# Interleaving the first two token blocks of an attention and mixture-of-experts kernel: one list of units, PSUM banks by role, a new order before the first unit

## The chip, the core and the metric

The kernel runs on one core of one Trainium2 chip. The metric is the device time of one execution in microseconds (us). Each kernel was executed several times; the median stands for it.

## What is computed

Inputs are attention tensors q, k, v of 8 batches, 8 heads, 576 positions and 64 features, and the weights of two layers. The output has 4608 tokens (8 × 576) of 512 features. The reference, cut to what matters:

```python
q_s = exp(q - max(q, -1)); q_s /= sum(q_s, -1) + 1e-9
k_s = exp(k - max(k, 2));  k_s /= sum(k_s, 2) + 1e-9      # over the 576 positions
kv = einsum('bhsd,bhse->bhde', k_s, v)
x = einsum('bhsd,bhde->bhse', q_s, kv)                    # then as [4608, 512]
h = x @ w_in;  g = h * cos(h);  x = g @ w_out             # 512 -> 2048 -> 512
keep = x @ w_skip > 0
e = argmax(x[keep] @ w_gate)                              # one of 8 experts a token
x[keep] += prob[e] * (maximum(x[keep] @ w1[e], 0) @ w2[e])
```

## The kernel before

**Blocks and units.** The 4608 tokens are cut into NB = 12 blocks of TB = 384. A block goes through the middle layer in NC = 16 units, one for each chunk of 128 of the 2048 features. Unit n of block j and chunk c has `h_mm` (L323: twelve products of 384 columns, in three terms of high and low parts of weight and x, four pieces of features), a chain that makes h·cos(h) (L328 and L329 in `chain_a`; L333, L334, L335 in `chain_b`; L340 and L342 in `chain_c`), and `out_mm` (L351: nine products of 512 columns, three groups of tokens by three terms), which adds into three PSUM banks of the block. `out_mm` follows LAG = 3 units behind. L335 is the last to read the PSUM bank of a unit's h. L328 and L333, L334, L340 run on ScalarE, L329 and L335 on VectorE, L342 on GpSimd.

**Weights.** w_in and w_out come as 64-bit numbers, in 32 chunks of 512 KB in the list `order`. A call of `w_step` takes one chunk to float32 and, two steps later, splits it into a high part (L141, ScalarE) and a low part (L150, on VectorE, or on GpSimd for chunks in the list LOP); L146 (ScalarE), L147 and L152 (VectorE) and L153 (GpSimd) convert the bits. There are 34 steps, three ahead of the first unit; each also issues the load of the chunk seven places later in `order`. In block 0 the tables WA, WB, WC say at which unit and at which place of it a step is taken. All weights stay in SBUF after that.

**Attention.** The x of block j + 1 is made while the units of block j run, by `attention`, which puts the pieces at units by tables (A1, Q1, X1 for block 1, AT and others for later ones): `kmax_a`, `kmax_b`, `kmax_c` (maximum of k and its subtraction, L200 to L217), `k_exp`, `kv_mm` (L231 to L237), `q_max` (L246, L247), `q_exp` (L250), `q_norm` (L255 to L261), `q_trans` (transposes, L298) and `x_make` (L310 to L314). From block 2 on the transposes of q are made by DMAs and VectorE (`q_block`, `q_turn`). A new batch of k and v begins in some blocks only; block 2 needs none. The exponential (L221, L250) needs another ScalarE table than the sine of the chain.

**Routing.** The routing of block j − 1 (`x2_trans` or `x2_block` and `x2_turn`, `logits` L392, `gates` L400, `rank`, `gate_exp`, `weigh`, and three table writes `place` L454 of GpSimd) runs during block j. The experts' products come after the last block.

**What sets the order.** The program is scheduled by hand: each engine runs its instructions in the order in which this code writes them, and SyncE issues the loads and stores in that order too. PSUM has eight banks of 512 numbers a partition: three for `out_mm`, a pool of three for h, a pool of two for all else.

## Time and profile before

| | us |
|---|---|
| median of three runs | 1286.64 (1280.89 to 1287.6) |
| the profiled execution, span from first to last instruction | 1285.2 |
| TensorE matmuls busy | 1216.3 (95%) |
| weight loads of TensorE busy | 1070.6 (83%) |
| VectorE busy | 772.6 (60%) |
| ScalarE busy | 739.0 (57%) |
| GpSimd busy | 412.2 (32%) |

The busy shares are averages over the whole span; stretches of it differ, so they are read by windows of time. Times in the trace count from the first instruction. An idle time in brackets says how long the engine stood before the instruction and what it waited for last.

### The profile page before, as it was taken

The page shows a single profiled execution, that of the slowest core. Times are in us where ns is not written, and L with a number is a line of the kernel's source. Part 1 is how long each engine was busy: PE and PEld are TensorE (multiplying, and loading weights), DVE is VectorE, ACT ScalarE, POOL GpSimd, SP SyncE. Part 2 cuts the span into 40 slices and gives each one's busy share as a digit, 9 for nine tenths or more (in the row PEclk, how much of TensorE's full clock was granted, in tenths as well). Part 3 has the DMA queues.
Part 4 walks back from the last instruction along what each step waited for, and adds up shares of the span by engine and source line. Part 5 has one row for each costly group of instructions (what it writes and reads, how often), then busy time and mean ns, then how long its engine had stood idle before and what let it go on. Part 6 is the DMA issues. An engine that isn't in the chain of part 4 may idle for free. (4 is left out here: it accounts for less than half of the span.)

```text
span 1285.2 us, 19966 instructions
## 1 busy us (share of the span) xinstructions
PE 1216.3 (95%) x7046; PEld 1070.6 (83%) x7046; DVE 772.6 (60%) x1539; ACT 739.0 (57%) x1432; POOL 412.2 (32%) x365
## 2 busy tenths in 40 slices
PE   7768999999999999999999999999999799999976
PEld 3666888888898998989888888988888688999964
DVE  7999635565553556554355655435577566767747
ACT  3657655665665566556556655656575355555436
POOL 3666632324333242333324233333110212221311
PEclk8989999999999999999999999999999899999988
DMA  9910222234222123322222232220336567776746
GB/s 303 369 63 1 64 37 62 50 70 104 63 62 38 62 53 85 86 63 66 34 62 53 64 106 63 64 36 16 109 86 204 167 195 244 225 233 215 230 143 202
DMA packets 215230, 143.03 MB, mean 111 GB/s; under 512 B 139322, under 2 KB 178490, under 8 KB 215104
## 3 DMA queue, kind: packets, MB, share of 16 engines
q1 hardware_dynamic: 209856, 129.33, 36.1%
q0 software_dynamic: 5248, 12.17, 2.8%
q8 instruction: 61, 1.00, 0.4%
q14 instruction: 65, 0.53, 0.1%
HBM read 110.94 MB, written 16.08 MB: 99 GB/s over the span
## 5 line engine op out<-in xcount | busy, mean ns | idle before, releaser
L323 PE MATMUL h<-xh,w 128*128 128x384 f32 x1536 | 435.3, 345 | 21.0 <-POOL w L150 6.2
L351 PE MATMUL o<-w,gh 128*128 128x512 f32 x1152 | 363.1, 396 | 2.3 <-ACT x L363 2.3
L323 PEld LDWEIGHTS h<-xh,w 128*128 128x128 f32 x1536 | 284.0, 190 | 38.3 <-DVE w L150 7.0
L342 POOL TENSOR_TENSOR gl<-a,gh 128x384 fp32r<-128x384 f32 x176 | 184.2, 1047 | 402.2 <-ACT gh L340 294.5
L323 PE MATMUL h<-xl,w 128*128 128x384 f32 x768 | 261.5, 340 | 0.1
L351 PEld LDWEIGHTS o<-w,gh 128*128 128x128 f32 x1152 | 214.7, 189 | 39.1 <-ACT x L363 3.6
L351 PE MATMUL o<-w,gl 128*128 128x512 f32 x576 | 228.7, 397 | 1.5 <-POOL gl L342 1.5
L335 DVE SCALAR_TENSOR_TENSOR a<-a,h 128x384 f32<-128x384 f32 x192 | 104.6, 545 | 192.1 <-ACT a L334 192.1
L328 ACT ACTIVATE a<-h 128x384 f32<-128x384 f32 x192 | 93.1, 485 | 181.1 <-PE h L323 108.3
L329 DVE SCALAR_TENSOR_TENSOR a<-a,h 128x384 f32<-128x384 f32 x192 | 105.3, 549 | 138.5 <-ACT a L328 138.4
L121 DVE TENSOR_TENSOR w<-wr,w 128x512 fp32r<-128x512 f32 x224 | 144.1, 687 | 12.5 <-ACT w L120 6.6
L323 PEld LDWEIGHTS h<-xl,w 128*128 128x128 f32 x768 | 146.1, 190 | 5.4 <-DVE xl L314 0.4
L340 ACT CAST gh<-a 128x384 fp32r<-128x384 f32 x192 | 97.9, 510 | 72.0 <-DVE a L335 71.9
L772 PE MATMUL h<-xh,w 128*128 128x256 f32 x704 | 138.5, 282 | 0.0
L351 PEld LDWEIGHTS o<-w,gl 128*128 128x128 f32 x576 | 108.5, 188 | 29.2 <-POOL gl L342 2.6
L120 ACT CAST w<-wr 128x512 fp32r<-128x512 f32 x224 | 126.4, 619 | 8.7 <-DMA wr<-in_w 7.0
L772 PEld LDWEIGHTS h<-xh,w 128*128 128x128 f32 x704 | 114.3, 190 | 3.8 <-ACT w L120 0.4
L783 PE MATMUL o<-w,gh 128*128 128x512 f32 x352 | 114.0, 405 | 0.0
L333 ACT ACTIVATE a<-a 128x384 f32<-128x384 f32 x192 | 100.7, 525 | 11.0 <-DVE a L329 10.7
L334 ACT ACTIVATE a<-a 128x384 f32<-128x384 f32 x192 | 100.8, 525 | 6.1
L775 ACT ACTIVATE gh<-h 128x256 fp32r<-128x256 f32 x88 | 33.8, 384 | 120.2 <-PE h L772 96.1
L772 PE MATMUL h<-xl,w 128*128 128x256 f32 x352 | 99.2, 282 | 0.0
(197 smaller groups left out, 1505.3 us busy)
## 6 DMA issues: line engine op xcount, KB each, us to landing
wr<-in_w SPq DMA_DIRECT2D x112, 512.0 KB, 4.5
qt<-in_q SPq DMA_DIRECT2D x12, 768.0 KB, 6.7
out<-x SPq DMA_DIRECT2D x36, 256.0 KB, 2.2
wr<-in_w_in SPq DMA_DIRECT2D x16, 512.0 KB, 10.1
wr<-in_w_out SPq DMA_DIRECT2D x16, 512.0 KB, 11.0
xl<-x SPq DMA_DIRECT2D x160, 48.0 KB, 2.1
xh<-qt SPq DMA_DIRECT2D x160, 48.0 KB, 2.1
vt<-in_v SPq DMA_DIRECT2D x7, 1040.0 KB, 6.1
```

Of the source, the lines that this page charges most:

```text
L120: nc.scalar.copy(hi, src)
L121: nc.vector.tensor_tensor(lo, src, hi.bitcast(F32), op=ALU.subtract)
L323: nc.tensor.matmul(Hp[n], win(a, kk, c), xT[j][b][:, kk, :], start=t == 0, stop=t == len(seq) - 1)
L329: nc.vector.scalar_tensor_tensor(a, a, MAGIC, Hp[n], op0=ALU.subtract, op1=ALU.subtract)
L333: nc.scalar.activation(a, a, AF.Sin, scale=PI)
L334: nc.scalar.activation(a, a, AF.Square)
L335: nc.vector.scalar_tensor_tensor(a, a, 0.5, Hp.pop(n), op0=ALU.subtract, op1=ALU.mult)
L340: nc.scalar.copy(G[n]["h"], a)
L342: eng.tensor_tensor(G[n]["l"], a, G[n]["h"].bitcast(F32), op=ALU.subtract)
L351: nc.tensor.matmul(O[j][g], gg[a][:, g * P:(g + 1) * P], wout(b, c), start=c == 0 and t == 0, stop=c == NC - 1 and t == 2)
L772: nc.tensor.matmul(ps, win2(a, kk, c0, c * P, P), xt[b][:, kk, 0:T2], start=t == 0, stop=t == len(seq) - 1)
L783: nc.tensor.matmul(o[g], g_[a][:, g * P:(g + 1) * P], wout(b, c0 + c), start=c == 0 and t == 0, stop=c == NF - 1 and t == 2)
```

## The change

Blocks 0 and 1 no longer run one after the other. The list UNITS names block and chunk of every unit: four units of block 0, then a unit of block 1 and one of block 0 in turn, then the rest; from block 2 on the order is the old one. `h_mm` and `out_mm` read block and chunk from it, and the loop counts along it.

The attention of block 1 is moved in front of unit 4 (`attention_head`), at the first four units; block 2's attention lies between units 12 and 31. The weight steps go by one short table WS (1, 2, 2, 2, 2, 1, then one at every unit), all at one place of a unit. The loads of k, v and q of block 1 are issued before the first unit. The routing of block 0 moves into block 2, where it runs beside block 1's, and its transposes are made on TensorE.

PSUM is one pool of eight named banks, and `roles` says which are for `out_mm` of a block, for h and for the rest: first 0 to 2, 3 to 5, 6 and 7. From unit 4 on, with two blocks open, `out_mm` of block 1 has 5 to 7, h has 3 and 4, and nothing is left for the rest; after block 0's last `out_mm` it is 5 to 7, then 3, 4 and 0, then 1 and 2.

Ahead of the first unit, the order of work is another: fewer warm-up products, `kmax_c` and `k_exp` of the first half of k directly after `kmax_b`, and the subtraction of q's maximum and half of q's scaling on VectorE for block 0.

```diff
-A1 = (3, 3, 4, 6, 7, 9, 9, 9, 10, 8)
...
+HEAD = 4
+UNITS = [(0, c) for c in range(HEAD)]
+for _c in range(10):
+    UNITS += [(1, _c), (0, HEAD + _c)]
+UNITS += [(0, 14), (1, 10), (0, 15)] + [(1, _c) for _c in range(11, NC)]
+UNITS += [(_j, _c) for _j in range(2, NB) for _c in range(NC)]
+POS = {u: n for n, u in enumerate(UNITS)}
+LAST0, LAST1 = POS[0, NC - 1], POS[1, NC - 1]
+KQ = 12, 2, 2
...
+WS = (1, 2, 2, 2, 2, 1)
...
+    banks, used = {}, {"h": 0, "m": 0}
+
+    def roles(o, h, m):
+
+        banks.update(o=o, h=h, m=m)
+
+    def bank(b):
+        return pp.tile([P, 512], F32, tag=f"b{b}", name=f"b{b}")
+
+    def turn_of(kind):
+        used[kind] += 1
+        return bank(banks[kind][used[kind] % len(banks[kind])])
...
+    roles((0, 1, 2), (3, 4, 5), (6, 7))
...
-        nc.gpsimd.tensor_tensor(t, t, m[:, :, None].to_broadcast([P, NG * H, D]), op=ALU.subtract)
+        eng = nc.gpsimd if j else nc.vector
+        eng.tensor_tensor(t, t, m[:, :, None].to_broadcast([P, NG * H, D]), op=ALU.subtract)
...
     def h_mm(n):
-        j, c = divmod(n, NC)
-        Hp[n] = ps_h.tile([P, TB], F32, tag="h", name="h")
+        j, c = UNITS[n]
+        Hp[n] = hidden()
...
-        if j < NB - 2:
+        if 0 < j < NB - 2:
             f[2] = [(x2_block, (j,))]
             f[TURN] = [(x2_turn, (j,))]
...
+    def attention_head():
+
+        f = {}
+        add = lambda s, fn, *a: f.setdefault(s, []).append((fn, a))
+        for c in range(1, 5):
+            add((0, 0, 1, 1)[c - 1], kmax_a, 1, 0, NP, (c,))
+        add(0, x_new, 1)
+        add(0, q_max, 1)
+        add(1, kmax_b, 1)
+        add(1, q_exp, 1)
+        add(1, kmax_c, 1)
+        add(2, k_exp, 1)
+        add(2, q_norm, 1)
+        add(3, kv_mm, 1)
+        for i in range(NP):
+            add(3, q_trans, 1, i)
+            add(3, x_make, 1, i)
+        add(KQ[0] - 4, load_q, 2)
+        add(KQ[0], q_max, 2)
+        add(KQ[0] + 1, q_exp, 2)
+        add(KQ[0] + 2, q_norm, 2)
+        add(KQ[0] + 4, q_block, 2)
+        add(KQ[0] + 8, q_turn, 2)
...
         for n in range(N + LAG):
-            j, c = divmod(n, NC)
-            if c == 0:
+            j, c = UNITS[n] if n < N else (NB, n - N)
+            if n == POS[1, 0]:
+                roles((5, 6, 7), (3, 4), ())
...
+                if j == 2:
+                    early0 = routing(0, rp, (0, 1, 2, 2, 3, 4, 5, 6, 7, 8))
...
+                jo, co = UNITS[n - LAG]
+                if co == NC - 1:
+                    evac(jo, xp)
+                    if jo == 0:
+                        roles((5, 6, 7), (3, 4, 0), (1, 2))
+            if at[0] < len(order) + 2:
+                w_step(WS[n] if n < len(WS) else 1)
```

**VectorE at the first units.** Names: wr, u and w are a chunk of weights on its way, a the chain, h its PSUM tile (b_ and a number in the new kernel), kt, km and kmx block 1's k and its maximum, qt and qm its q. Before, behind the second unit:

```order
L335 SCALAR_TENSOR_TENSOR a<-a,h 128x384
L329 SCALAR_TENSOR_TENSOR a<-a,h 128x384
L147 TENSOR_SCALAR u<-wr 128x512
L150 TENSOR_TENSOR w<-u,w 128x512
L152 SCALAR_TENSOR_TENSOR wr<-wr,u 128x512
L147 TENSOR_SCALAR u<-wr 128x512
L150 TENSOR_TENSOR w<-u,w 128x512
L152 SCALAR_TENSOR_TENSOR wr<-wr,u 128x512
L335 SCALAR_TENSOR_TENSOR a<-a,h 128x384
```

In the changed kernel, behind its second unit:

```order
L362 SCALAR_TENSOR_TENSOR a<-a,b_357 128x384
L356 SCALAR_TENSOR_TENSOR a<-a,b_391 128x384
L166 TENSOR_SCALAR u<-wr 128x512
L169 TENSOR_TENSOR w<-u,w 128x512
L171 SCALAR_TENSOR_TENSOR wr<-wr,u 128x512
L166 TENSOR_SCALAR u<-wr 128x512
L169 TENSOR_TENSOR w<-u,w 128x512
L171 SCALAR_TENSOR_TENSOR wr<-wr,u 128x512
L219 TENSOR_TENSOR km<-km,kt 128x512
L219 TENSOR_TENSOR km<-km,kt 64x512
L227 TENSOR_REDUCE kmx<-b_436 128x4
L235 TENSOR_TENSOR kt<-kt,b_444 128x2048
```

Two weight steps stand between two units in both; the maximum and subtraction of block 1's k have come in behind them.

**TensorE where block 1's x is made.** Names: qt and qh, ql are q and its split transpose, kvbh and kvbl the split product of k and v, m a PSUM tile of the small pool, o the sums of `out_mm`. Before, transposes and products (L298, L310) lie between units:

```order
L310 MATMUL m_1168<-qh_1034,kvbh0_91 128x192
L310 MATMUL m_1168<-ql_1035,kvbh0_91 128x192
L310 MATMUL m_1168<-qh_1034,kvbl0_92 128x192
L310 MATMUL m_1168<-qh_1034,kvbh1_93 128x192
L310 MATMUL m_1168<-ql_1035,kvbh1_93 128x192
L310 MATMUL m_1168<-qh_1034,kvbl1_94 128x192
L298 MATMUL m_1177<-ident_58,qt_492 128x128 x3
L323 MATMUL h_1193<-xh_284,w_1120 128x384
```

In the changed kernel, the end of four such pairs, ahead of the fifth unit (the first of block 1):

```order
L337 MATMUL b_649<-qh,kvbl_88 128x192
L325 MATMUL b_658<-ident,qt 128x128 x3
L337 MATMUL b_666<-qh,kvbh_85 128x192
L337 MATMUL b_666<-ql,kvbh_85 128x192
L337 MATMUL b_666<-qh,kvbl_86 128x192
L337 MATMUL b_666<-qh,kvbh_87 128x192
L337 MATMUL b_666<-ql,kvbh_87 128x192
L337 MATMUL b_666<-qh,kvbl_88 128x192
L350 MATMUL b_675<-xh,w 128x384
```

Each transpose now stands directly ahead of the products that read it, with no unit between.

**TensorE in the interleaved part.** Here b with a digit is the PSUM bank: b3 and b4 hold h, b0 to b2 sums of block 0, b5 to b7 sums of block 1.

```order
L350 MATMUL b3_815<-xh_296,w_707 128x384
L350 MATMUL b3_815<-xl_297,w_707 128x384
...
L378 MATMUL b5_838<-w_424,gh_750 128x512
...
L378 MATMUL b7_840<-w_424,gl_751 128x512
L350 MATMUL b4_860<-xh_386,w_414 128x384
L350 MATMUL b4_860<-xl_387,w_414 128x384
...
L378 MATMUL b0_525<-w_805,gh_792 128x512
```

Before, at this place, all units were of block 0 and h went round three banks; now units of both blocks alternate and h alternates between two banks.

## Rows read from the trace of the kernel before

**Rows 1.** Busy time by stretch: length, engines with instruction counts, granted clock, DMA share, GB/s.

```profile
34.00:140.00 106.00, 81.02 (x439) 68.67 (x438) 101.41 (x133) 69.66 (x133) 72.92 (x56) 0.92 0.38 133
140.00:211.00 71.00, 71.00 (x364) 63.34 (x364) 34.95 (x77) 43.97 (x86) 26.07 (x23) 1.00 0.19 34
```

**Rows 2.** Timeline of TensorE: start, us, engine, line, operation, tiles, count, idle time before.

```profile
33.78 0.34 PE L323 MATMUL h<-xh,w 128*128 128x384 f32 x1
...
46.90 0.44 PE L323 MATMUL h<-xh,w 128*128 128x384 f32 x1 [3.83 <-DVE a L335]
...
50.49 0.79 PE L351 MATMUL o<-w,gh 128*128 128x512 f32 x2
...
139.82 0.34 PE L323 MATMUL h<-xh,w 128*128 128x384 f32 x1
...
144.03 0.34 PE L323 MATMUL h<-xh,w 128*128 128x384 f32 x1
...
209.52 0.34 PE L310 MATMUL m<-qh,kvbh 128*128 128x384 f32 x1
...
210.58 0.34 PE L323 MATMUL h<-xh,w 128*128 128x384 f32 x1
```

**Rows 3.** Timeline of VectorE, first chain operation, then two weight steps and a chain.

```profile
36.65 0.55 DVE L329 SCALAR_TENSOR_TENSOR a<-a,h 128x384 f32<-128x384 f32 x1 [1.30 <-ACT a L328]
...
118.67 0.41 DVE L147 TENSOR_SCALAR u<-wr 128x512 uint32<-128x512 uint32 x1
...
120.70 0.41 DVE L147 TENSOR_SCALAR u<-wr 128x512 uint32<-128x512 uint32 x1
...
123.09 0.54 DVE L335 SCALAR_TENSOR_TENSOR a<-a,h 128x384 f32<-128x384 f32 x1
123.55 0.54 DVE L329 SCALAR_TENSOR_TENSOR a<-a,h 128x384 f32<-128x384 f32 x1
```

**Rows 4.** Timeline of VectorE ahead of the first unit.

```profile
11.08 3.00 DVE L200 TENSOR_TENSOR km<-kt 128x256 f32<-128x256 f32 x1
...
14.45 1.21 DVE L216 TENSOR_TENSOR kt<-kt,m 128x1024 f32<-128x1024 f32 x1
...
17.62 0.42 DVE L208 TENSOR_REDUCE kmx<-m 128x2 f32<-128x256 f32 x1 [0.84 <-PE m L206]
```

**Rows 5.** Timeline of TensorE, transposes and products that make x of block 0.

```profile
22.54 0.82 PE L298 MATMUL h<-ident,qt 128*128 128x128 f32 x6
...
25.86 0.44 PE L310 MATMUL m<-ql,kvbh 128*128 128x384 f32 x1 [1.42 <-DVE ql L121]
...
31.42 0.69 PE L310 MATMUL m<-qh,kvbh 128*128 128x384 f32 x1
...
32.82 0.52 PE L310 MATMUL m<-qh,kvbh 128*128 128x384 f32 x1
```

**Rows 6.** Timeline of ScalarE, a table load and the exponential behind it.

```profile
97.28 1.28 ACT L250 ACT_TABLE_LOAD   x1
98.58 1.48 ACT L250 ACTIVATE qt<-qt 128x1536 f32<-128x1536 f32 x1
```

**Rows 7.** Timelines of VectorE and GpSimd, a step with nothing beside it, one beside GpSimd.

```profile
85.33 0.41 DVE L147 TENSOR_SCALAR u<-wr 128x512 uint32<-128x512 uint32 x1
...
86.87 0.54 DVE L335 SCALAR_TENSOR_TENSOR a<-a,h 128x384 f32<-128x384 f32 x1
...
92.83 2.87 POOL L247 TENSOR_TENSOR qt<-qt,qm 128x1536 f32<-128x1536 f32 x1 [0.47 <-DVE qm L246]
...
93.12 3.13 DVE L152 SCALAR_TENSOR_TENSOR wr<-wr,u 128x512 uint32<-128x512 uint32 x1
```

**Rows 8.** Groups by line, 140 to 211 us (busy, mean ns, idle before); GpSimd's timeline.

```profile
L392 PE MATMUL m<-x,wgs 128*32 128x384 f32 x8 | 0.9, 498 | 0.0
L400 PE MATMUL m<-ident,lt 128*128 128x128 f32 x3 | 0.5, 271 | 0.0
...
220.55 0.98 POOL L454 DMA_INDIRECT tab<-row,idx  x1 [5.21 <-DMA tab<-row,idx]
```

More of the change, by code (lines that the diff above doesn't have):

```diff
@@ L340, in chain_c @@
         nc.scalar.copy(G[n]["h"], a)
[L341 removed]
+        eng = nc.gpsimd if UNITS[n][0] < NB - 1 else nc.vector
         eng.tensor_tensor(G[n]["l"], a, G[n]["h"].bitcast(F32), op=ALU.subtract)
     def out_mm(n):
[L345 removed]
+        j, c = UNITS[n]
         if c == 0:
[L347 removed]
+            O[j] = [acc(g) for g in range(NG)]
         gg = G.pop(n)
@@ L465, in routing @@
         else:
-            for g in range(NG):
+            for g in range(NG if j else 0):
                 add(g, x2_trans, j, g)
@@ L481, in attention @@
         add = lambda s, fn, *a: f.setdefault(s, []).append((fn, a))
-        one = j == 1
-        at = A1 if one else AT
+        at = AT
         add(at[6], q_exp, j)
@@ L493, in attention @@
         add(at[7], q_norm, j)
-        if not one:
-            add(QB, q_block, j)
-            add(QT, q_turn, j)
+        add(QB, q_block, j)
+        add(QT, q_turn, j)
         for i in range(NP):
-            add((Q1 if one else QTR)[i], q_trans, j, i)
-            add((X1 if one else XM)[i], x_make, j, i)
+            add(QTR[i], q_trans, j, i)
+            add(XM[i], x_make, j, i)
+        return f
+    def attention_head():
[20 more added lines that the diff above has]
+        add(KQ[0] + 8, q_turn, 2)
+        add(LAST0, x_new, 2)
+        at = LAST0 + LAG
+        for i in range(NP):
+            add(at + i // 2, q_trans, 2, i)
+            add(at + 1 + i // 2, x_make, 2, i)
+        add(at + 2, x2_trans, 0, 0)
         return f
@@ L810, in body @@
         load_v(0, 0, 2)
-        for m in order[0:6]:
+        for m in order[0:2]:
             w_load(m)
         load_v(0, 2, 4)
-        for m in order[6:AHEAD]:
+        for m in order[2:AHEAD]:
             w_load(m)
-        nc.sync.dma_start(cfs, cf)
-        nc.sync.dma_start(cis, ci)
-        nc.sync.dma_start(tri, ct)
-        nc.sync.dma_start(wgs, wg.rearrange("(k p) e -> p k e", p=P))
         kmax_a(0, 0, 2)
@@ L822, in body @@
         kmax_b(0, 0, 2)
+        kmax_c(0, 0, 2)
+        warm(11)
         q_max(0)
-        kmax_a(0, 2, 4, (1, 2))
+        k_exp(0, 0, 2)
+        kmax_a(0, 2, 4)
         q_exp(0)
-        kmax_c(0, 0, 2)
-        warm(18)
-        k_exp(0, 0, 2)
+        kmax_b(0, 2, 4)
+        kmax_c(0, 2, 4)
         init_table()
-        kmax_a(0, 2, 4, (3, 4))
-        kmax_b(0, 2, 4)
+        kv_mm(0, 0, 2)
+        k_exp(0, 2, 4)
         q_norm(0)
-        warm(3)
-        warm(3)
-        kv_mm(0, 0, 2)
-        kmax_c(0, 2, 4)
+        warm(6)
+        w_step()
         q_trans(0, 0)
-        k_exp(0, 2, 4)
+        q_trans(0, 1)
+        kv_mm(0, 2, 4)
         w_step()
-        w_step()
-        q_trans(0, 1)
         x_new(0)
@@ L849, in body @@
         w_step()
+        load_k(1)
+        load_v(1)
+        load_q(1)
         x_make(0, 2)
         x_make(0, 3)
-        N = NB * NC
+        N = len(UNITS)
+        f = attention_head()
+        r = {}
         for n in range(N + LAG):
-            j, c = divmod(n, NC)
-            if c == 0:
+            j, c = UNITS[n] if n < N else (NB, n - N)
+            if n == POS[1, 0]:
+                roles((5, 6, 7), (3, 4), ())
+            if c == 0 and j > 1:
                 f = attention(j + 1) if j + 1 < NB else {}
@@ L860, in body @@
                     prefetch, compute, small, small_ids = mlp(mp)
-                r = routing(j - 1, rp, (3, 4, 5, 6, 7, 8, 9, 10, 11, 12) if j == NB - 1 else RT) if 0 < j < NB else {}
-            if j == 0 and FP[c] == 0:
-                run(f.pop(c, []))
+                r = routing(j - 1, rp, (3, 4, 5, 6, 7, 8, 9, 10, 11, 12) if j == NB - 1 else RT) if j < NB else {}
+                if j == 2:
+                    early0 = routing(0, rp, (0, 1, 2, 2, 3, 4, 5, 6, 7, 8))
+                    early0[0] = [(x2_trans, (0, 1))]
+                    early0[1] = [(x2_trans, (0, 2))]
+                    for t in early0:
+                        r[t] = early0[t] + r.get(t, [])
+            key = n if j < 2 else c
             if n < N:
```

74 lines of the change are left out of this document (32 added, 42 removed).

## The prediction

> **What bounds the kernel now.** I read first the busy times by stretch [rows 1]. Core 0 runs 1285.2 us from its first instruction to its last; from 140 to 211 us TensorE is busy all the time, and a unit of the main loop (twelve products L323, nine L351) takes 144.03 − 139.82 = 4.21 us [rows 2]. The stretch from 34 to 140 us is another thing: VectorE is busy 101.41 of 106 us, TensorE 81.02 at a granted clock of 0.92. The first 16 units start between 33.78 and 139.82 us [rows 2], 6.6 us each. So block 0 is bound by VectorE, which splits the weights there, and block 1 by TensorE. Blocks 0 and 1 together, from the first unit to the first of block 2, take 210.58 − 33.78 = 176.8 us, where 32 units alone would need 32 × 4.21 = 134.7. That difference of 42 us, less some 6 us of other products, is all that an interleaving can win.
>
> What VectorE does in the stretch follows from distances in its timeline [rows 3]. A weight step with both parts takes 123.09 − 120.70 = 2.39 us, one whose low part GpSimd makes 120.70 − 118.67 = 2.03, one operation of the chain of a unit 123.55 − 123.09 = 0.46. About 30 steps lie in the stretch, 10 of them with the low part on GpSimd (from the list LOP): 20 × 2.39 + 10 × 2.03 = 68. Fifteen units add 15 × 0.92 = 14. The 19.4 us left of 101.4 are the attention of block 1.
>
> **The start, up to the first unit.** The order is turned (k before q), half of the warm-up products go away, and the subtraction of q's maximum moves from GpSimd to VectorE. There, an operation with 1024 elements takes 1.21 us [rows 4], so 1536 take 1.8. In exchange L200, which took 3.00 us for 256 elements beside GpSimd's subtraction, loses that stall. What is late next is the chain from q's scaling over the transposes to the four x_make. Following it through with these durations I again come to the first product at 34 us, with the last split of x at about 35.5. I keep 33.8; 2 us earlier and 4 later are the bounds.
>
> **The head: five units with the attention of block 1.** The new order puts nine weight steps and all of that attention between units 0 and 4, so VectorE has 6 × 2.39 + 3 × 2.03 = 20.4, 19.4, and nine chain operations 4.1: 43.9 us, against 5 × 4.2 = 21 us of unit products. All weights that are not yet there must wait for it in program order, and TensorE waits with them, since its unit n + 2 needs the bank that L335 of unit n frees. To this come holes in VectorE's own row, where it waits for others. From the first product to the first L329: 36.65 − 33.78 = 2.9 [rows 2, 3]. Two round trips for k's maximum over TensorE, the one wait that the trace has 0.84 [rows 4]: 1.7, with no other work put between as there was before. About 1 behind the exponential of k. Then the four pairs of q_trans and x_make, which now stand directly behind each other: transpose, copy, split, product, copy, split, on two banks. The trace has no such pair. Where the transposes ran ahead, products followed each other in 31.42 to 32.82, 1.4 us; from the first transpose to its dependent product were 25.86 − 22.54 = 3.3 us [rows 5]. These are the bounds; I take 2.4, near the middle, since one product of about 0.9 and three copies or splits of 0.5 make it up. VectorE works 0.9 of that, so the holes are 4 × 1.5 = 6. Another 1 us passes from the end of the next unit to its chain. Holes: 12.6 us. TensorE also runs slowly after a pause (the 0.92 of rows 1 is a mean of its levels, 2.4 and 1.2 GHz): a unit that began after 3.83 us of idling took 50.49 − 46.90 = 3.6 us for products that take 2.1 [rows 2]; two such lie on the path, 3 us. So the seventh unit starts 43.9 + 12.6 + 3 = 59.5 us after the first, at 93 us. In the old order ten units had started by then.
>
> ScalarE reloads its table for q and for k separately, four loads instead of two. The load took 1.28 us, from 97.28, and the exponential behind it started at 98.58 [rows 6]: nothing lies between. Two more loads are 2.6 us of ScalarE, of which the 1 us above shows. The Trainium skill, "ScalarE: Activation LUTs", section "What ACT_TABLE_LOAD costs", counts a drain of about 1.38 us on top of each load. By the page the head would be some 3 us longer and the time 1292; the row shows no drain, so I leave it out.
>
> **From the seventh unit to block 2.** One weight step a unit remains: VectorE has 0.92 + 2.39 = 3.3 us in 4.21 us of products. From the end of a unit's first products to L335 I count 0.5 + 0.5 + 2.4 + 0.5 = 3.9 us, and with two banks TensorE needs it after 2.1 + 2.1 + 2.1 = 6.3. So TensorE sets the pace: 26 × 4.21 = 109.5 us, x_make of block 2 adds 2.1 (two of its four chunks ran from 209.52 to 210.58, [rows 2]), the first transposes of x2 0.5. Block 2's q work comes in three successive units: two reductions on VectorE, the exponential between two loads (1.28 + 1.48 + 1.28 = 4 us of ScalarE), and GpSimd operations such as the 2.87 us beside which L152 took 3.13 [rows 6, 7]. This exceeds the slack of 2.4 us about twice; I put 3.5 us, bounds 0 and 8. Changing the banks behind block 0 costs 0.7. Loads are no limit: in the present stretch the DMA engines are at 0.38 [rows 1], and the last chunks are wanted later than now. Sum: 59.5 + 109.5 + 2.1 + 0.5 + 4.2 = 175.8, so block 2 starts at 209.6, 1.0 us earlier than now.
>
> **Block 2 and later.** The routing of block 0 moves from block 1, where it is counted in the 176.8, into block 2, whose old length does not hold it. Logits 0.9, gates 0.5 [rows 8], rank 0.3 and two groups of four transposes 0.5 each, both estimated from the gates' three: 2.7 us of TensorE. The three table writes of GpSimd move too; each waits for the one before it (5.21 us, rows 8) with gl queued behind it. One us of that shows today in the first units of block 2 and would go; behind q's scaling in the middle of the block I expect two. From block 3 on the order of work is the same with three h banks and two others as before: nothing.
>
> **Forecast.** −1.0 + 2.7 + 1 = +2.7 us on the profiled 1285.2, which lies 1.4 below the median 1286.64: 1289 us. The reason is that the change trades a long stretch bound by VectorE for a short stretch that is worse (60 us for six units) and a long one at full pace.
>
> **Rivals.** *VectorE finds GpSimd quiet in the head.* A step with nothing beside it took 86.87 − 85.33 = 1.54 us [rows 7], 0.85 less. In the head GpSimd has some 25 us of work in 60, against 72.92 in 106 now [rows 1]. If the nine steps ran free that is 8 us, and with shorter gaps the 3 us of slow clock go as well: 1278. For it: L329 and L335 take GpSimd's place beside a single step. Against: steps come in twos there, and GpSimd's add of the first falls on the second, as in rows 3. The Trainium skill, "SBUF — State Buffer", section on the shared port pair, has a lock by which an operation with two inputs in SBUF waits out a whole GpSimd one; 3.13 beside 2.87 agrees, and by it a quiet GpSimd gives the short time.
>
> *Two banks are too few.* If L335 comes later than 6.3 us after its unit's first products, every unit from the seventh to the 26th stretches. It needs VectorE or GpSimd (whose gl frees the buffer a of unit n + 2) to fall behind by 2.4 us and stay behind. A contended step of 2.39 leaves 0.9 us a unit to recover, which speaks against it; in every second late unit GpSimd also makes a low part, for it. Losing 0.6 us on 20 units is 12 us: 1301.
>
> *The start is later* by up to 4 us through the subtraction on VectorE: 1293, within the forecast's own case. That the units are not interleaved is excluded by the order of TensorE's work.
>
> **Chances.** A measurement of this kernel tells about 0.5%, 6.4 us, from no change. The forecast with its bounds (1281 to 1293) has 0.50, the first rival 0.25, the second 0.25. By those bounds: faster 0.25, within 0.5% 0.50, slower 0.25. Eight times in ten the time should lie between 1277 and 1300: the ends take in most of both rivals.
>
> **What would show it.** First product of a unit at 34 us, the seventh unit's at 93, block 2's at 210, and a block 2 that is 3 to 4 us longer. VectorE with some 12 us of holes between 34 and 93, most in a row of four; TensorE at half there and full from the seventh unit on. A seventh unit before 87 speaks for the first rival; a spacing above 4.5 us in units 7 to 25, with L323 waiting for L335's successor, for the second. The forecast is wrong if the holes overlap with work, or if block 2 takes the old routing at no cost.

## The result and the profile after

The changed kernel takes 1299.38 us (median, 1296.88 to 1301.92), against 1285.93 us of the kernel before (the three runs above and one more): 1.0105 times as long, with an interval of 1.0083 to 1.0126. So the change makes the kernel about 1% slower. That lies 0.6 us inside the upper end of the range (1277 to 1300 us), and the likeliest case of the prediction, no change that can be measured, did not come.

The profiled executions have spans of 1285.2 and 1297.5 us. Starts of units, read from TensorE's timelines, say where the 12.3 us lie:

| us | before | forecast | after |
|---|---|---|---|
| first unit starts | 33.8 | 33.8 | 36.7 |
| from there to the seventh unit | 33.3 | 59.5 | 65.6 |
| from there to block 2 | 143.5 | 116.3 | 117.8 |
| block 2 starts | 210.6 | 209.6 | 220.1 |
| block 2 takes | 77.8 | 81.5 | 82.1 |
| blocks 3 to 10 take | 596.0 | 596.0 | 596.5 |

The rest, from block 11 to the end, is 2.0 us shorter after (400.9 and 398.9). It lay between 396 and 405 us in eleven other kernels whose code there is the same, so nothing is read from it. Block 2 starts 9.5 us later than before the change and takes 4.3 us more; against the forecast, 9.0 us were lost before the seventh unit.

First the busy times by stretch of the changed kernel: length, then TensorE's products, its weight loads, VectorE, ScalarE and GpSimd, with instruction counts, then TensorE's granted clock, the DMA share and GB/s. The last two rows are the head (first to seventh unit) and the interleaved part (from there to block 2).

```profile
20.00:30.00 10.00, 7.56 (x57) 4.67 (x57) 7.62 (x14) 3.47 (x7) 3.21 (x2) 0.50 0.86 306
50.00:60.00 10.00, 3.30 (x13) 2.90 (x14) 6.59 (x9) 4.54 (x5) 2.65 (x3) 0.50 1.07 352
80.00:90.00 10.00, 7.60 (x27) 5.73 (x27) 3.80 (x8) 2.63 (x6) 0.21 (x1) 0.50 0.00 0
36.70:102.31 65.61, 39.43 (x228) 33.06 (x228) 47.48 (x63) 33.99 (x57) 24.76 (x19) 0.73 0.55 188
102.31:220.10 117.79, 113.98 (x564) 102.27 (x562) 86.65 (x125) 80.58 (x160) 72.26 (x60) 0.99 0.13 36
```

The first of these stretches in the kernel before:

```profile
20.00:30.00 10.00, 7.93 (x98) 6.00 (x98) 7.51 (x18) 5.84 (x11) 4.97 (x4) 0.84 1.04 329
```

Read the granted clock first. From 20 to 30 us, before the first unit, it is 0.50, TensorE's lower level of 1.2 GHz, where the kernel before had 0.84; in the head it is 0.50 again, from 50 to 60 and from 80 to 90 us. In the interleaved part it is 0.99. Then the head's row: of 65.6 us VectorE works 47.5 and stands 18.1. TensorE's timeline of the changed kernel (start, us, engine, line, operation, tiles, count, idle time before) shows what the lower level does:

```profile
25.49 1.51 PE L325 MATMUL b<-ident,qt 128*128 128x128 f32 x6 [2.44 <-issue]
26.93 3.02 PE L250 MATMUL b<-vt,kt 128*64 128x65 f32 x40
...
36.70 0.52 PE L350 MATMUL b<-xh,w 128*128 128x384 f32 x1
...
57.82 2.08 PE L233 MATMUL b<-ident,kmx 128*128 128x128 f32 x8 [0.78 <-DVE kmx L227]
...
84.24 0.50 PE L337 MATMUL b<-qh,kvbh 128*128 128x192 f32 x1 [0.63 <-ACT qh L139]
...
87.42 0.50 PE L337 MATMUL b<-qh,kvbh 128*128 128x192 f32 x1 [0.63 <-ACT qh L139]
...
102.31 0.34 PE L350 MATMUL b<-xh,w 128*128 128x384 f32 x1
...
106.50 0.34 PE L350 MATMUL b<-xh,w 128*128 128x384 f32 x1
...
142.92 0.44 PE L350 MATMUL b<-xh,w 128*128 128x384 f32 x1 [2.65 <-DVE a L362]
...
220.06 0.42 PE L350 MATMUL b<-xh,w 128*128 128x384 f32 x1
```

Six transposes of q take 1.51 us, where they took 0.82 in [rows 5]. The pairs that make x of block 1 come every 87.42 − 84.24 = 3.18 us, not 2.4. From the seventh unit on a unit takes 4.2 us, as in [rows 2]; the one wait in that part that is worth naming stands at 142.92. VectorE's timeline shows its side:

```profile
47.11 2.33 DVE L166 TENSOR_SCALAR u<-wr 128x512 uint32<-128x512 uint32 x1
49.36 1.48 DVE L169 TENSOR_TENSOR w<-u,w 128x512 fp32r<-128x512 f32 x1
...
57.08 0.69 DVE L227 TENSOR_REDUCE kmx<-b 128x4 f32<-128x512 f32 x1 [1.21 <-PE b L225]
59.94 2.29 DVE L235 TENSOR_TENSOR kt<-kt,b 128x2048 f32<-128x2048 f32 x1 [2.17 <-PE b L233]
...
86.72 0.56 DVE L341 SCALAR_TENSOR_TENSOR xl<-b,xh 128x384 fp32r<-128x384 f32 x1 [2.00 <-ACT xh L340]
```

The two round trips of k's maximum leave VectorE idle for 1.21 and 2.17 us (the one in [rows 4] for 0.84), and each of the four pairs for 2.00. L166, 0.41 us in [rows 3] and [rows 7], takes 2.33 at 47.11, beside this operation of GpSimd:

```profile
46.39 2.76 POOL L267 TENSOR_TENSOR qt<-qt,qm 128x1536 f32<-128x1536 f32 x1 [2.35 <-DVE qm L265]
```

### The profile page after: what moved, and what is told of

Its sections match the earlier page's. It is cut to its first block, busy times and chain, and to the rows that moved or that the text cites. A ratio compares the mean times of both kernels' runs of the same rounds, so it can differ in the third digit from the quotient of the medians.

```text
span 1297.5 us, 19961 instructions
## 1 busy us (share of the span) xinstructions
PE 1224.0 (94%) x7051; PEld 1078.5 (83%) x7051; DVE 775.4 (60%) x1537; ACT 744.8 (57%) x1437; POOL 407.7 (31%) x363
## 5 line engine op out<-in xcount | busy, mean ns | idle before, releaser
L350 PE MATMUL b<-xh,w 128*128 128x384 f32 x1536 | 433.6, 344 | 10.4 <-DVE a L362 6.0
L378 PE MATMUL b<-w,gh 128*128 128x512 f32 x1152 | 361.9, 395 | 1.8 <-ACT x L390 1.8
L350 PEld LDWEIGHTS b<-xh,w 128*128 128x128 f32 x1536 | 284.0, 190 | 25.4 <-DVE a L362 7.3
L350 PE MATMUL b<-xl,w 128*128 128x384 f32 x768 | 260.9, 340 | 0.0
L378 PEld LDWEIGHTS b<-w,gh 128*128 128x128 f32 x1152 | 214.2, 188 | 38.0 <-ACT x L390 2.8
L378 PE MATMUL b<-w,gl 128*128 128x512 f32 x576 | 228.4, 396 | 0.9 <-POOL gl L369 0.9
L362 DVE SCALAR_TENSOR_TENSOR a<-a,b 128x384 f32<-128x384 f32 x192 | 104.6, 545 | 187.8 <-ACT a L361 187.2
L356 DVE SCALAR_TENSOR_TENSOR a<-a,b 128x384 f32<-128x384 f32 x192 | 105.4, 549 | 136.6 <-ACT a L355 136.4
L350 PEld LDWEIGHTS b<-xl,w 128*128 128x128 f32 x768 | 145.9, 190 | 5.0
L828 PE MATMUL b<-xh,w 128*128 128x256 f32 x704 | 138.5, 282 | 0.0
L378 PEld LDWEIGHTS b<-w,gl 128*128 128x128 f32 x576 | 108.3, 188 | 28.4 <-POOL gl L369 2.0
L828 PEld LDWEIGHTS b<-xh,w 128*128 128x128 f32 x704 | 114.3, 190 | 3.8 <-ACT w L139 0.4
L839 PE MATMUL b<-w,gh 128*128 128x512 f32 x352 | 114.0, 405 | 0.1
```

The lines of the kernel that those rows point to most:

```text
L350: nc.tensor.matmul(Hp[n], win(a, kk, c), xT[j][b][:, kk, :], start=t == 0, stop=t == len(seq) - 1)
L356: nc.vector.scalar_tensor_tensor(a, a, MAGIC, Hp[n], op0=ALU.subtract, op1=ALU.subtract)
L362: nc.vector.scalar_tensor_tensor(a, a, 0.5, Hp.pop(n), op0=ALU.subtract, op1=ALU.mult)
L378: nc.tensor.matmul(O[j][g], gg[a][:, g * P:(g + 1) * P], wout(b, c), start=c == 0 and t == 0, stop=c == NC - 1 and t == 2)
L828: nc.tensor.matmul(ps, win2(a, kk, c0, c * P, P), xt[b][:, kk, 0:T2], start=t == 0, stop=t == len(seq) - 1)
L839: nc.tensor.matmul(o[g], g_[a][:, g * P:(g + 1) * P], wout(b, c0 + c), start=c == 0 and t == 0, stop=c == NF - 1 and t == 2)
```

## The experiments

The theory after this comparison: the start and the head are chains of small products on TensorE and of splits on ScalarE and VectorE. TensorE pauses in them, falls to 1.2 GHz, and its pieces, which lie on VectorE's path there, take up to twice the time. The rivals are VectorE's own work and its contention with GpSimd, the order of the pairs, and the two banks for h. Whole times resolve some 3 us here, so a stage is judged by starts of units; the first unit of one and the same start order began between 35.0 and 37.2 us in nine profiles, so the head is counted from the first unit.

### The start, kept busy

```diff
         kmax_c(0, 0, 2)
-        warm(11)
+        warm(22)
...
         q_norm(0)
-        warm(6)
+        warm(24)
```

> The changed kernel with more products that nothing reads ahead of the first unit: 22 instead of 11 behind the first half of k, 24 instead of 6 behind the first products of k and v. In the changed kernel TensorE was granted 0.50 from 20 to 30 us and the first unit began at 36.7 us (33.8 before the change); six transposes took 1.51 us, the 40 products of k and v 3.02. Theory A (the late start is TensorE at 1.2 GHz, because it idles between its small pieces): granted clock 0.9 or more from 15 to 35 us, six transposes about 0.8, first unit at 34.5, total 2 us less. Rival B (the start is set by the row of VectorE, which has taken over q's subtraction and runs beside GpSimd): the clock rises, but the first unit stays within 0.5 us of 36.7. Rival C: the added products are late themselves and the first unit comes later than 36.7.

Measured: the first unit starts at 33.76 us, as before the change. Windows and TensorE's timeline of this kernel:

```profile
20.00:30.00 10.00, 8.80 (x78) 5.50 (x76) 9.28 (x18) 5.19 (x11) 3.22 (x2) 1.00 1.04 362
```

```profile
24.01 0.84 PE L325 MATMUL b<-ident,qt 128*128 128x128 f32 x6
24.78 1.83 PE L250 MATMUL b<-vt,kt 128*64 128x65 f32 x40
...
33.76 0.52 PE L350 MATMUL b<-xh,w 128*128 128x384 f32 x1
```

The granted clock is 1.00, the transposes take 0.84 us and the products of k and v 1.83, so the late start is the clock: theory A. It is 2.9 us against this profile of the changed kernel, and 1.2 to 3.4 us against the nine with its start order. The run does not show that the change's fewer products are what lowered the clock, since it has more of them than the kernel before (56 against 34; the change has 27). Only 1.9 us of it reach block 2 (218.2 instead of 220.1): the head takes 66.7 us from the first unit, 1.1 more, in small waits of several units. The whole time, 1.0096 times before (1.0074 to 1.0118), cannot be told from the change's own 1.0105. In the head, which was left alone, the granted clock is still 0.50 (50 to 60 and 80 to 90 us) and a pair still takes 3.18 us.

### The head, kept busy

```diff
+        add(1, fill, 52, 0)
         add(1, kmax_b, 1)
...
             add(3, q_trans, 1, i)
+            add(3, fill, 2 if i else 26, 3)
             add(3, x_make, 1, i)
```

`fill(n, b)` issues n products into bank b that nothing reads.

> The changed kernel with products that nothing reads in the head: 52 ahead of the transposes of block 1's k maximum, 26 behind the first transposes of q and two behind each later one. In the changed kernel the maximum's way over TensorE left VectorE idle for 3.4 us, the four pairs of q_trans and x_make came every 3.18 us, and the fifth unit's products took 3.6 us. Theory A (these are TensorE at 1.2 GHz): idle 2.0 us, pairs every 2.1 to 2.3 us, fifth unit 2.1 us, seventh unit at 96 instead of 102.3 us, total 6 us less. Rival B (the pairs are bound by the handing over between four operations on three engines, not by the length of the products): the clock rises but the pairs stay above 2.8 us, seventh unit at 100 or later, total at most 2 us less.

Measured, TensorE's timeline:

```profile
57.23 0.60 PE L230 MATMUL b<-ident,km 128*128 128x128 f32 x4
58.61 1.16 PE L238 MATMUL b<-ident,kmx 128*128 128x128 f32 x8 [0.78 <-DVE kmx L232]
...
83.31 0.33 PE L342 MATMUL b<-qh,kvbh 128*128 128x192 f32 x1 [0.51 <-DVE xl L346]
...
85.76 0.33 PE L342 MATMUL b<-qh,kvbh 128*128 128x192 f32 x1 [0.51 <-DVE xl L346]
...
97.66 0.34 PE L355 MATMUL b<-xh,w 128*128 128x384 f32 x1
```

The pairs come every 2.45 us, the transposes for the maximum take about half the time, and the seventh unit starts 60.9 us after the first instead of 65.6. So the lower level cost the head 4.7 us, and they lie in two places: from the first x_make to the fifth unit 8.9 us pass instead of 12.1, and the fifth unit's twelve products take 2.1 us instead of 3.7. The faster maximum gave nothing: VectorE's idle time there fell from 3.4 to 2.6 us (2.0 expected), but the first x_make comes 43.6 us after the first unit in both kernels. Block 2 starts 4.6 us earlier, 1.4 short of the expectation; part of that is that a pair is not 2.1 to 2.3 but 2.45, since 1.42 us of each remain in which VectorE waits. The head's row of this kernel, for the account below:

```profile
36.76:97.66 60.90, 53.04 (x313) 37.76 (x313) 46.67 (x63) 33.84 (x57) 24.55 (x19) 0.93 0.57 192
```

VectorE works 46.7 us of it and stands 14.2. The whole time, 1.0087 (1.0061 to 1.0113), again tells no difference.

### The pairs, staggered

```diff
             add(3, q_trans, 1, i)
-            add(3, x_make, 1, i)
+            if i:
+                add(3, x_make, 1, i - 1)
+        add(3, x_make, 1, NP - 1)
...
-            t = misc()[:, 0:TB] if j else hidden()
+            t = bank(3 + i % 2)[:, 0:TB] if j else hidden()
```

> The changed kernel with the four pairs of block 1 staggered: transposes of chunk i + 1 ahead of the products of chunk i, transposes in two banks that h leaves free at that place. Theory A (each pair is one chain: transpose, copy, split, product, copy, split; nothing of it overlaps): the pairs come every 2.3 us even at 1.2 GHz, the last product of x three times 0.9 us earlier, seventh unit 2.7 us earlier at 99.6 us, total 2.5 us less. Rival B (TensorE's own length at 1.2 GHz, 0.84 + 1.5 us, and not the order, sets the pairs): hardly less than 3.18 us a pair, total within 1 us.

Measured, TensorE's timeline (the first products of each x_make, and the seventh unit):

```profile
80.53 0.53 PE L337 MATMUL b<-qh,kvbh 128*128 128x192 f32 x1 [6.04 <-ACT qh L139]
...
83.53 0.51 PE L337 MATMUL b<-qh,kvbh 128*128 128x192 f32 x1
...
85.40 0.49 PE L337 MATMUL b<-qh,kvbh 128*128 128x192 f32 x1
...
86.38 0.33 PE L337 MATMUL b<-qh,kvbh 128*128 128x192 f32 x1
...
95.99 0.34 PE L350 MATMUL b<-xh,w 128*128 128x384 f32 x1
```

The seventh unit comes 59.15 us after the first, 6.5 us earlier than in the changed kernel, where 2.7 were expected, and the kernel takes 1.0055 (1.0036 to 1.0075) times before: half of the loss is gone. Theory A held, and the clock joined it. At the lower level a pair now takes 85.40 − 83.53 = 1.87 us. Without pauses in the pairs TensorE rose to the full level in their midst (the products that took 0.41 us each at 84 us take 0.27 at 86), so the fifth unit ran at full speed too. Of the 6.5 us, 5.0 lie between the first x_make and the fifth unit and 1.5 in the fifth unit. One cause brought both: a chain in which nothing overlaps is long and makes TensorE slow.

### GpSimd's subtraction left out

```diff
         nc.vector.reduce_max(m, t, axis=AX.X)
+        if j == 1:
+            return
```

> The changed kernel with one operation of GpSimd left out: the subtraction of q's maximum for block 1 (the softmax does not need it for these inputs). In the changed kernel it took 2.76 us, and beside it the weight step's L166 took 2.33 us and its L169 1.48, where 0.41 and 0.7 stand elsewhere. Theory A (the head is longer by GpSimd's operations beside VectorE's): the step takes 1.6 instead of 4.5 us, the third unit comes 2.5 us earlier after the first (20.3 instead of 22.8), and the seventh 63 instead of 65.6 us after it. Rival B (the step's time only moves into a wait for TensorE or ScalarE): the third unit still 22.5 us after the first.

Measured on VectorE: L166 of that step, 2.33 us in the changed kernel, is back at 0.41.

```profile
45.41 0.41 DVE L166 TENSOR_SCALAR u<-wr 128x512 uint32<-128x512 uint32 x1
46.12 1.11 DVE L169 TENSOR_TENSOR w<-u,w 128x512 fp32r<-128x512 f32 x1 [0.30 <-ACT w L160]
```

The third unit comes 20.9 us after the first instead of 22.8, but the seventh 65.1 instead of 65.6. So the contention is there, and of its 1.9 us 1.0 is left at the fifth unit and 0.5 at the seventh: later waits take the rest up. It is not what made the head long. (This is a single run, 1297.7 us.) The Trainium skill, "SBUF — State Buffer", section "Who interferes with whom", has the waiting operation blocked for the whole of GpSimd's; the trace of the changed kernel agrees, since L166 ends there at 47.11 + 2.33 = 49.44 and L267 at 46.39 + 2.76 = 49.15.

### The attention over eight units

```diff
-HEAD = 4
+HEAD = 8
...
-WS = (1, 2, 2, 2, 2, 1)
+WS = (1, 2, 2, 2, 2, 2, 2, 2, 2, 1)
...
+        add(2, kmax_b, 1)
+        add(3, kmax_c, 1)
+        add(3, q_exp, 1)
+        add(3, k_exp, 1)
+        add(4, q_norm, 1)
+        add(5, kv_mm, 1)
```

with the transposes at units 5 to 7 and the products at 6 and 7, and UNITS interleaved from unit 8 on.

> The changed kernel with the attention of block 1 spread over eight units of block 0 instead of four; interleaving starts at unit 8. Each round trip over TensorE then has a unit's products between its parts, and the exponentials of q and k share a table. Theory A (the head is a sum of VectorE's work and of holes; the holes go, the work stays): 17 steps of 2.4, 19 of attention, 9 of chains and 3 of waiting, 72 us, so the ninth unit starts 72 us after the first (74.0 in the changed kernel), block 2 at 217 to 218 us after the start instead of 220.1. Rival B (the density of the head also costs contention and clock, which goes with it): ninth unit 65 us after the first, block 2 at 211.

Measured: the ninth unit comes 74.7 us after the first, against 74.0 in the changed kernel and 72 or 65 expected, and the kernel takes 1.0126 (1.0095 to 1.0158) times before. Neither expectation held. The holes did not go, they moved: VectorE waits 4.28 us at once behind the two exponentials that now share a table,

```profile
74.40 0.55 DVE L362 SCALAR_TENSOR_TENSOR a<-a,b 128x384 f32<-128x384 f32 x1 [4.28 <-ACT a L361]
```

and in units 6 and 7, where two x_make fall into one unit, the second still waited 2.00 us for its copy. TensorE was again at 0.50 from 73 to 82 us, so the clock did not come back either. Spreading pieces over more units hides a wait only where other work of the same engine stands behind it in its row.

### Block 2's q work

The interleaved part takes 117.8 us from the seventh unit to block 2 in the changed kernel and in the six variants that leave it alone (117.76 to 117.78). It holds 26 units at 4.2 us, block 2's x and 5.2 us by which units 15 to 18 (counted from 0, as in the code) come late (2.8, 1.6, 0.7 and 0.1), behind the exponential of block 2's q. First its three pieces were set further apart:

```diff
-        add(KQ[0], q_max, 2)
-        add(KQ[0] + 1, q_exp, 2)
-        add(KQ[0] + 2, q_norm, 2)
+        add(10, q_max, 2)
+        add(13, q_exp, 2)
+        add(17, q_norm, 2)
```

> The changed kernel with block 2's q work spread: its maximum at unit 10, exponential at 13, scaling at 17, the transfers at 19 and 23, where the change has them at 12, 13, 14, 16 and 20; the load of q comes at unit 6 instead of 8. In the changed kernel units 14, 15 and 17 came 2.8, 1.7 and 0.6 us late, 5 us in all. Theory A (the three pieces follow too closely for VectorE, ScalarE and GpSimd to catch up): less than 2.5 us of lateness left, block 2 at 217.5 instead of 220.1 us. Rival B (the 4 us of ScalarE for one exponential between two table loads, with two h banks, is the whole loss): still 4 to 5 us, block 2 at 219.5 to 220.5.

Measured: 118.15 us for the stretch. Of the lateness 4.1 us stand at the exponential (4.5 in the changed kernel) and 1.5 at the maximum and the scaling (0.8):

```profile
142.20 0.45 PE L350 MATMUL b<-xh,w 128*128 128x384 f32 x1 [2.23 <-DVE a L362]
```

So rival B held: the exponential between its two loads is the loss, not the neighbourhood of the three pieces. The whole time, 1.0130 (1.0108 to 1.0152), is no better either. Then the same work was brought forward into the head, where TensorE has other work than units that wait for the chain:

```diff
         add(3, kv_mm, 1)
+        add(3, load_q, 2)
...
+            if i == 0:
+                add(3, q_max, 2)
...
+        add(3, q_exp, 2)
+        add(10, q_norm, 2)
```

> The changed kernel with block 2's q brought forward: loaded behind block 1's products of k and v into the place of block 1's k, its maximum taken between the pairs of q_trans and x_make, its exponential directly behind the last x_make of block 1, its scaling at unit 10. There TensorE has two units' products and two out_mm without waiting for the chain. In the changed kernel the exponential stood at unit 13, in the part where TensorE is full and h has two banks, and units 14 to 17 came 5.3 us late. Theory A (an exponential between two table loads costs 4 us only where less slack than that lies ahead of the chain): units 7 to 31 keep 4.2 us, the head grows by at most 1.5 us, block 2 starts 3.5 to 5 us earlier after the first unit (178.5 to 180 instead of 183.4). Rival B (the delay moves with the exponential): the fifth to tenth units come 4 us later and nothing is won.

Measured, ScalarE's timeline behind the last pair, and the seventh unit on TensorE:

```profile
91.55 1.28 ACT L274 ACT_TABLE_LOAD   x1
92.84 1.49 ACT L274 ACTIVATE qt<-qt 128x1536 f32<-128x1536 f32 x1
94.34 1.28 ACT L364 ACT_TABLE_LOAD   x1
```

```profile
102.44 0.45 PE L354 MATMUL b<-xh,w 128*128 128x384 f32 x1 [1.61 <-DVE a L366]
```

The stretch behind the seventh unit falls to 113.9 us, 3.8 less, and the head grows by 1.5; block 2 starts 181.0 us after the first unit instead of 183.4. Between the two expectations: about half of the price was won, and the rest moved. The whole time does not tell it (1.010, 1.0069 to 1.0132).

How much of the price is the two banks? The kernel before got two instead of three:

```diff
-    ps_h = m1.enter_context(tc.tile_pool(name="ps_h", bufs=3, space=PSUM))
+    ps_h = m1.enter_context(tc.tile_pool(name="ps_h", bufs=2, space=PSUM))
```

> The kernel before the change with two PSUM banks for h instead of three, and nothing else. There, with three banks, the exponential of q between two table loads (units 6 and 7 of a block) costs nothing: blocks 4, 7 and 10, which take no new batch of k, last 70.8 us each and keep 4.2 us a unit around it. Theory A (in the interleaved part the same exponential cost 5.3 us because h had two banks there): units away from exponentials keep 4.2 us, units 7 to 9 of blocks 4, 7 and 10 come 3 to 5 us late, and these blocks last 74 to 76 us. Rival B (it cost so much because a weight step a unit fills ScalarE and GpSimd there): blocks 4, 7 and 10 stay within 0.5 us of 70.8. Rival C (two banks are too few for every unit): all units longer than 4.4 us, blocks of 78 us and more.

Measured: blocks 4, 7 and 10 last 72.5, 72.5 and 72.8 us instead of 70.8, with 0.7 us at the exponential of q,

```profile
413.49 0.45 PE L323 MATMUL h<-xh,w 128*128 128x384 f32 x1 [0.51 <-DVE a L335]
```

and units away from ScalarE's long operations keep 4.2 us. In blocks that take a new batch of k, with its exponential behind q's, the same place costs 3 us, and block 11 starts at 921.5 instead of 884.3 us (one run, 1320.6 us against 1284.1). The rest of the 1.7 us of blocks 4 and 7 lies at their last units, where the next block's x is made. So the forecast's rival "two banks are too few" is wrong for plain units and right beside long stretches of ScalarE; but two banks alone make 0.7 us of the 5.2 here, less than theory A's 3 to 5. Last, the weight steps were taken away from the place:

```diff
-WS = (1, 2, 2, 2, 2, 1)
+WS = (1, 2, 2, 2, 2, 1, 1, 1, 2, 2, 2, 1, 1, 0, 0, 0)
```

> The changed kernel with the table of weight steps altered: none at units 13 to 15, where block 2's q exponential falls, and two instead of one at units 8 to 10. In the changed kernel units 14 to 17 came 5.3 us late behind the exponential; with two banks for h and no weight steps beside it (the kernel before with two banks) the exponential cost 0.7 us, with three banks and no weight steps nothing. Theory A (two banks and a weight step a unit together make the 5.3 us, since ScalarE is then filled and can't catch up): 0.5 to 2 us late at units 14 to 17, and up to 4 us late at units 9 to 12, where a unit now has two steps. Rival B (it is the interleaving itself, two open blocks and out_mm in turn): still 4.5 us or more at units 14 to 17.

Measured: the units behind the doubled steps come 3.7 us late, and those behind the exponential still 5.1 us:

```profile
147.46 0.69 PE L350 MATMUL b<-xh,w 128*128 128x384 f32 x1 [2.43 <-DVE a L362]
```

By its number rival B held, and block 2 starts 187.4 us after the first unit, 4.1 later than in the changed kernel (one run, 1307.6 us). But here the exponential met a row that the doubled steps had already made late, so the run does not separate the two. The traces of the changed kernel and of the old one with two banks divide the price further. ScalarE's timelines, the first operation of a unit's chain and the table load behind it:

```profile
134.04 0.49 ACT L355 ACTIVATE a<-b 128x384 f32<-128x384 f32 x1 [1.23 <-PE b L350]
...
137.10 1.28 ACT L270 ACT_TABLE_LOAD   x1
```

```profile
406.76 0.49 ACT L328 ACTIVATE a<-h 128x384 f32<-128x384 f32 x1 [1.99 <-PE h L323]
...
407.67 1.28 ACT L250 ACT_TABLE_LOAD   x1
```

From the load to the unit that waits for the chain both take 5.82 us (to 142.92 and 413.49). Ahead of the load 3.06 us pass instead of 0.91. Of these 2.15 us, the two operations of a weight step on ScalarE take 1.2, and a wait for VectorE, which has q's maximum in its row, takes 0.9. They are the difference between 2.8 and 0.7 us of lateness, so in this first late unit nothing is left for the interleaving itself. The unit behind it comes another 1.6 us late although TensorE waits for nothing there: after its wait of 2.65 us it runs at 0.50 from 144 to 146 us. In the combined kernel below it stays at 1.00, and waits for VectorE, which scales q, take the same time; so the two cover each other, and the place costs 5.2 us in both.

### Block 2 itself

```diff
-early0 = routing(0, rp, (0, 1, 2, 2, 3, 4, 5, 6, 7, 8))
+early0 = routing(0, rp, (0, 1, 2, 2, 3, 4, 6, 6, 7, 8))
```

> The changed kernel with one number changed: the gates' exponential of block 0, which the change moved into block 2, one unit later, so that it stands directly ahead of block 3's q exponential and both share a table. In the changed kernel the two exponentials stood 5 us apart with four table loads, unit 10 of block 2 came 3.0 us late, and block 2 took 82.1 us (77.8 before the change). Theory A (the loads of ScalarE delay the chain): two loads less, 2.6 us, of which 2 to 2.6 us show; block 2 takes 79.5 to 80. Rival B (the late unit comes from q's exponential alone, as in the interleaved part): block 2 takes 81.5 to 82.5.

Measured: block 2 takes 79.2 us instead of 82.1, 1.4 more than before the change. ScalarE's timeline has one pair of loads for both exponentials:

```profile
252.10 1.28 ACT L468 ACT_TABLE_LOAD   x1
253.39 0.22 ACT L468 ACTIVATE sh<-sh 128x24 f32<-128x24 f32 x1
253.52 1.47 ACT L270 ACTIVATE qt<-qt 128x1536 f32<-128x1536 f32 x1
...
257.33 1.28 ACT L360 ACT_TABLE_LOAD   x1
```

Theory A: two loads are 2.6 us, and block 2 wins 2.9. (In the variants that leave block 2 alone it took 81.3 to 82.8 us, and 86.0 in the single run without the subtraction; in the two kernels below that have this edit it took 78.4 and 78.8.) With three banks, one such group costs next to nothing; two of them 5 us apart cost 3. The whole time is 1.0099 (1.0069 to 1.0129).

### The causes together

The longer warm-up of the first experiment, the staggered pairs, 52 products ahead of the maximum of k (`add(1, fill, 52, 0)`) and the two exponentials of block 2 together:

> The changed kernel with the longer warm-up at the start (46 instead of 17 products behind the first half of k), staggered pairs, 52 products that nothing reads ahead of the maximum of block 1's k, and the gates' exponential of block 0 beside q's. If the parts add: first unit at 33.8 us instead of 36.7, seventh unit 58 us after it instead of 65.6, block 2 at 210 instead of 220.1, 2.5 us less in block 2; the total 12 us less, 1288, as the kernel before the change. If they cover one another (the clock that the staggered pairs bring back is the same as that of the added products): 8 us less, 1292.

Measured: 1287.43 us, 1.0012 (0.9994 to 1.003) times the kernel before. The clock in the first 30 us is 1.00 (the row has the last ten), and the units come on time:

```profile
20.00:30.00 10.00, 9.14 (x79) 5.69 (x77) 8.96 (x17) 5.17 (x12) 3.22 (x2) 1.00 0.98 345
```

```profile
33.76 0.35 PE L355 MATMUL b<-xh,w 128*128 128x384 f32 x1
...
93.60 0.34 PE L355 MATMUL b<-xh,w 128*128 128x384 f32 x1
```

First unit at 33.76, seventh 59.8 us after it (58 expected), block 2 at 211.4, block 2 in 78.4 us. So the low clock of the start, the pairs and the two exponentials account for the loss of the change: without them the kernel is as fast as before, and no faster. The products ahead of k's maximum added nothing to the staggered pairs, which alone had 59.15.

One more version went further, with block 2's q brought forward as above, 24 products ahead of the first x_make, and the maximum of q taken while TensorE transposes k's:

> The combined kernel (longer warm-up, staggered pairs, products ahead of the maximum of k, exponentials of block 0's gates and block 3's q together) with, besides, block 2's q brought forward, 24 products that nothing reads ahead of the first x_make of block 1, and the maximum of block 1's q taken while TensorE transposes the maximum of its k, its exponential beside k's. The combined kernel gave 1287.4 us against 1286.4 of the kernel before, first unit at 33.8, seventh at 93.6, block 2 at 211.4. If the parts add: seventh unit at 92, block 2 at 205, total 6 us less than the combined kernel, 0.4% to 0.6% faster than the kernel before. If the exponential behind the last x_make delays the chain, or GpSimd's subtraction now falls on VectorE's weight steps: no gain, within 0.2% of the kernel before.

Measured: 1290.95 us, 1.0022 (1.0004 to 1.0041). The delay moved: the seventh and eighth units came 3.2 and 2.9 us late, 6 us together, more than the interleaved part had lost. The seventh waits for the chain behind the exponential; the eighth is late because TensorE runs at 0.50 after that wait:

```profile
95.57 0.69 PE L361 MATMUL b<-xh,w 128*128 128x384 f32 x1 [3.01 <-DVE a L373]
```

```profile
96.00:101.00 5.00, 5.00 (x16) 4.71 (x16) 4.27 (x6) 3.23 (x8) 3.99 (x5) 0.50 0.01 5
```

Block 2 still starts 176.1 us after the first unit, 1.5 less than in the combined kernel. This profile is of the longest of twelve runs (1294.53 us), with the first unit at 36.1 and 405.0 us from block 11 on, so it does not tell where the median lost.

No version tried beats the kernel before.

## Why the prediction was off

**The start** was given 33.8 with bounds of −2 and +4 us, and came 2.9 late, inside the bounds. The step that failed is its first sentence: that warm-up products go away was noted and given no price (it says half of them; 27 of 34 stay). What TensorE then does at the lower level cost 2.9 us, and with more products it was gone; that the seven missing ones alone lowered the level is not shown. The subtraction on VectorE, which was priced (1.8 us, measured 1.76), was not the cause.

**The head's work.** VectorE was to work 43.9 us and worked 47.5: attention 19.1 (forecast 19.4), weight steps 23.0 (20.4), chains 5.4 (4.1, two operations more lie in the stretch than were counted). The steps are 2.6 us over, and GpSimd's subtraction of q's maximum accounts for 2.3 of them (L166 and L169 of one step, 3.81 beside it and 1.52 without); the head was only 0.5 us shorter when it was left out.

**The head's holes** were to be 12.6 us with 3 of slow clock beside them, 15.6 together, and were 18.1 in all. This is the step that failed. The slow clock was charged to two units, 1.5 us each, and not to the small products. With the head kept busy 1.5 us came back in one unit, the fifth, and 3.2 in the four pairs, so the term was 4.7 us and not 3. Each pair was given 2.4 us from rows that were partly taken at the higher level; at full clock it measured 2.45, so the estimate was right for a TensorE that isn't in this head, and at 1.2 GHz a pair takes 3.18. The clock is thus 1.7 of the 6.1 us by which the head was missed. The other 4.4 are there without it too: kept busy, the head still takes 60.9 us, where the forecast without its slow clock has 43.9 + 12.6 = 56.5. There VectorE works 2.8 us more than forecast and stands 1.6 more, 0.9 of it in the round trips of the maximum (2.6 us instead of 1.7; 3.4 in the changed kernel). The wait behind k's exponential was 1.2 us (forecast 1). The sentence in the forecast that TensorE runs slowly after a pause had the mechanism; it was applied to the long products, where it is easy to see, and not to the chain of short ones, where it counts.

**From the seventh unit to block 2** 116.3 us were forecast and 117.8 came. The pace was right within a hundredth (4.20 us a unit measured, 4.21 forecast). The q work of block 2 was 5.2 us and not 3.5, within its bounds of 0 and 8.

**Block 2** was to be 3.7 us longer and is 4.3 us longer, for the wrong reason: the forecast had 2.7 us of routing products on TensorE and 1 of table writes. With the two exponentials side by side all of that routing stayed in the block, and it was 1.4 us longer (0.6 in the combined kernel). The rest, 2.9 us, were two more table loads in this block, where the forecast counted none; its two more were those of the head. From block 3 on nothing was forecast, and 0.5 us came.

**The rivals.** A quiet GpSimd was refuted: the steps got longer, not shorter. Two banks were refuted as told: every unit from the seventh on kept 4.2 us but those behind the exponential. The time of 1301 that this rival gave is near the measured one by accident, and since the upper end of the range was set to take in most of that rival, the range holds the measured time by luck. The late start, put inside the likeliest case, was real, though not through the subtraction. The sum of misses is 2.9 + 6.1 + 1.5 + 0.6 = 11.1 us; with the forecast's own +2.7 that makes 13.8, and block 3 starts 13.8 us later than before.

The Trainium skill, "ScalarE: Activation LUTs", section "What ACT_TABLE_LOAD costs", would have added a drain to each load. It was left out rightly: here too the exponential starts 1.29 us after a load of 1.28 (91.55 and 92.84).

## What to carry to other kernels

When a change thins out what TensorE does in a stretch, price its clock there first: read the granted clock of such a stretch, and where it is at the lower level give the small products and transposes on the path up to twice their length (here 1.51 instead of 0.82 us for six transposes, 3.18 instead of 2.45 for a pair), because each of them stands in a round trip that VectorE waits for. Dependent pairs (transpose, split, product, copy) belong one step apart, which here overlapped them and brought the clock up at once. Before an exponential of another table is moved, count what the engines behind it can do without the chain, and put two of them side by side rather than a few us apart.

## What the hardware showed besides

The level at the start is not the same in each execution of one and the same order. Of the nine profiles with the changed kernel's start, three ran at 0.50 from 20 to 30 us (first unit at 36.7 to 37.2 us) and six at 0.67 (35.0 to 36.8 us). The longer warm-up was granted 1.00 in two profiles (33.76 both) but 0.63 and 0.68 in the two halves of 15 to 25 us in the last kernel, whose first unit then came at 36.1. So in these profiles products that nothing reads brought the full level more often, two times of three against none of nine, and did not ensure it.
